# Convolution and ReGLU feed-forward: a smaller tap load spread by TensorE, constants moved to GpSimd, and zero matmuls between the first stages

## The chip, the cores and the metric

The kernel runs on one core of a Trainium2 chip. The metric is the device time of one execution in microseconds, as the median of several runs; lower is better. Durations and times of day inside the kernel come from one profiled execution and count from the start of its span.

## The reference

The input is `x` with 8 sequences of 4096 tokens and 192 channels, all in float32. There are two parts.

1. A causal convolution with 7 taps. The channels form 8 heads of 24; each head has its own 7 taps, which are the soft-max of a row of `weight` (8 rows of 7). Every token becomes the weighted sum of itself and the six tokens before it.
2. A feed-forward layer on all 32768 tokens: `gate = max(x @ w_gate, 0)`, `val = x @ w_val`, both 192 by 1536, and `out = (gate * val) @ w_out`, 1536 by 192.

```python
w = exp(weight - max(weight)); w = w / (sum(w) + 1e-09)
out = einsum('hk,bskhg->bshg', w, x_unfolded)
gate = maximum(x @ w_gate, 0.0)
val = x @ w_val
return gate * val @ w_out
```

## The kernel before

**Tiling.** Two sequences, `NB` = 4 apart, are worked on together as two streams: channels lie on partitions 0 to 63 for one and 64 to 127 for the other, in three chunks of 64 channels. A unit is 1024 tokens of both streams; there are 16 units. In each, `gate_val` runs twice (two windows of 512 tokens) over 12 slices of 128 columns of the two weight matrices: 12 matmuls into PSUM (L521), the relu on ScalarE (`gr`, L530) and the product on VectorE (`hT`, L531). Then `project_columns` multiplies by `Wo` (L541), VectorE turns the result (`turn_out`, L555) and SyncE stores it. The last unit uses `project` (L577) instead. PSUM is one ring of four tiles, all called `ps`.

**The convolution** is made in two ways. From unit 2 on it is done with the taps as per-partition scalars (the "lanes"): GpSimd loads x as float16 (`x_e`, L393), copies it into another order (`x_p`, L430), SyncE turns it with DMA transposes (`x_r`, L425 and L432), ScalarE makes products (`acc` L478, `prod` L458), VectorE accumulates (L489) and GpSimd adds (L467). This is worked on two units ahead: the lanes of unit 2 are made while unit 0 is projected. They need `tap`, the taps laid out by channel, which `load_taps` fills with 32 small DMAs on SyncE (L288) out of `wn`, the taps spread over 16 partitions per head.

For units 0 and 1 the convolution is a matmul with a band matrix. The tokens are cut into groups of up to five steps of 112. Group 0 (`conv_dense(0)`, L325) is on the way to the first gate; group 1 (`conv_dense(1)`) is done between the gates f = 9, 10 and 11 of unit 0; groups 2 and 3 (`conv`, L347) make unit 1.

**The start.** Group 0 of x is read as float32 by SyncE (`load_raw`, L111), one DMA per step in the order `STEPS0` = 1, 0, 2, 3, 4; these are the "raw steps". They are cast to float16 by `cast` (L121): steps 1, 0 and 2 on ScalarE, 3 and 4 on VectorE. The taps are read by ScalarE's queue (L129), with each of the 8 rows repeated for 16 partitions. VectorE and ScalarE make the soft-max (L221, L224, L239, L240) and from it `blocks` (L242). 16 small matmuls (L259) with shifted parts of `Z`, a 0/1 matrix, raise the blocks into the two halves of the band; VectorE copies out the first, ScalarE the second (L269). Ahead of this TensorE runs six matmuls on zeros (`WARM`, L175) and two that zero the band's PSUM (L180).

**Weights.** GpSimd loads both weight matrices in five slices (`load_w`, L198; columns 0, 128, 256, 512, 896 to 1536), cast to float16 on the way, into partitions 0 to 63. The copies to partitions 64 to 127 (`both_halves`, L205) are made by VectorE for slice 0, by GpSimd for slices 1 to 4 (`pool_halves`), and by two SyncE DMAs for the last 256 columns (they lie in load slice 4), at the head of `load_taps`.

**What sets the order.** Each engine takes its instructions in program order, and the order is written by hand. On SyncE it is: raw steps, the two weight copies of L205, the 32 tap loads, the transposes for `x_r`, the transposes for unit 1 (L379), stores. On GpSimd: constants, ten weight loads, the copies of slices 1 to 4 with the two x loads of group 1 (L94) between them, the x loads of group 2, `x_e`, `Wo`, and so on. A DMA waits for the one that had its semaphore before: each of SyncE and GpSimd has eight. VectorE's eviction of chunk 1 (L335) stands behind the copies of slice 0.

```python
for jj in STEPS0:
    for second in range(2):
        for st in range(2):
            for k2 in range(2): ...   # L325: x step (stationary) by band (moving)
copy = nc.vector.tensor_copy if c == 1 and g == 0 else nc.scalar.copy   # L334
```

Of the kernel before, what the change touches and what calls it, by code (L numbers as in the profile page):

```python
# [8 lines left out]
FP = mybir.dt.float32  # L9
F16 = mybir.dt.float16  # L10
ACTF = mybir.ActivationFunctionType
ALU = mybir.AluOpType
# [3 lines left out]
def kernel(  # L16
# [12 lines left out]
    nc = tc.nc  # L29

    B, S, D = x.shape
    H, KW = weight.shape
    G = D // H
    DFF = moe_w_gate.shape[1]
    PAD = KW - 1
# [7 lines left out]
    STEPS = [4, 5, 4]  # L43
    TAPS = [(6, 5, 4), (3, 2), (1, 0)]
    GSUB = 5
    WARM = 6
    STEPS0 = [1, 0, 2, 3, 4]
    CONV1 = [9, 10, 11]

# [12 lines left out]
    const = ctx.enter_context(tc.tile_pool(name="const", bufs=1))  # L62
# [7 lines left out]
    psum = ctx.enter_context(tc.tile_pool(name="psum", bufs=4, space=bass.MemoryType.PSUM))  # L70
# [5 lines left out]
    def staged(i, j):  # L76
        return stages[i][:, XH * j : XH * (j + 1)]

    def load_x(g, streams=range(2)):


        bp, toks = GROUPS[g]
        xt = staged(g // 3, g % 3).rearrange("p (j s d) -> p j s d", s=2, d=D)
        for st in streams:
            b = bp + NB * st
            last = toks[-1] == S - SUB or toks[-1] - toks[-2] != SUB
            n_full = len(toks) - int(last)
            lo = toks[0] - PAD
            src = bass.AP(
                tensor=x.tensor,  # L90
                offset=x.offset + (b * S + lo) * D,
                ap=[[D, 128], [SUB * D, n_full], [1, D]],
            )
            nc.gpsimd.dma_start(out=xt[:, 0:n_full, st, :], in_=src)  # L94
            if last:
                nc.gpsimd.dma_start(
                    out=xt[0 : SUB + PAD, len(toks) - 1, st, :],
                    in_=x[b, toks[-1] - PAD : toks[-1] + SUB, :],
                )
        return xt  # L100

    xts = {0: staged(0, 0).rearrange("p (j s d) -> p j s d", s=2, d=D)}
    ROWS = [SUB + PAD, 128, 128, 128, 80]
    raw = [
        apool.tile([128, FLAT - LDVE], FP, name=f"prod{jj + 1}")[:, 0 : 2 * D] for jj in range(GSUB)
    ]
# [13 lines left out]
    def cast(copy, jj):  # L120
        copy(  # L121
            out=xts[0][0 : ROWS[jj], jj, :, :].rearrange("p s d -> p (s d)"),
            in_=raw[jj][0 : ROWS[jj], :],
        )

    HR = 128 // H
    BW = HR + PAD
    w = const.tile([128, KW], FP)
    nc.scalar.dma_start(  # L129
        out=w[:],  # L130
        in_=bass.AP(tensor=weight.tensor, offset=weight.offset, ap=[[KW, H], [0, HR], [1, KW]]),
    )
    for jj in STEPS0:
        load_raw(jj)

    zeros = const.tile([128, 512], F16)
    nc.vector.memset(zeros[:], 0.0)
    e = const.tile([128, KW + 1], FP)
    nc.vector.memset(e[:, KW:], 1e-9)
    Z = const.tile([128, 256], F16)  # L140
    nc.vector.memset(Z[:], 0.0)
    nc.vector.memset(raw[0][0:PAD, :], 0.0)
    early = const.tile([128, 1], FP)
    nc.scalar.activation(out=early[:], in_=e[:, KW:], func=ACTF.Exp)

    ones = const.tile([128, 128], FP)
    nc.gpsimd.memset(ones[:], 1.0)
    eye = const.tile([128, 128], FP)
    nc.gpsimd.affine_select(
        out=eye[:],  # L150
        in_=ones[:],
        pattern=[[-1, 128]],
        compare_op=ALU.is_equal,
        fill=0.0,
        base=0,
        channel_multiplier=1,
    )
    mask = const.tile([128, H, 1], FP)
    with nc.allow_low_precision("one of the terms is not zero"):
        nc.vector.tensor_reduce(  # L160
            out=Z[:, 112 : 112 + HR],
            in_=eye[:].rearrange("p (g i) -> p i g", i=HR),
            axis=mybir.AxisListType.X,
            op=ALU.add,
        )
    nc.vector.tensor_reduce(
        out=mask[:, :, 0],
        in_=eye[:].rearrange("p (g i) -> p g i", i=HR),
        axis=mybir.AxisListType.X,
        op=ALU.add,  # L170
    )

    held = psum.tile([128, 2, 512], FP, name="ps")
    for _ in range(WARM):
        nc.tensor.matmul(  # L175
            out=held[:, 0, :], lhsT=zeros[:, 0:128], rhs=zeros[:], start=True, stop=True
        )
    raised = [psum.tile([128, 2, 512], FP, name="ps") for _ in range(2)]
    for half in range(2):
        nc.tensor.matmul(  # L180
            out=raised[half][:, 0, 0 : SUB * H // 2],
            lhsT=zeros[:, 0:128],
            rhs=zeros[:, 0 : SUB * H // 2],
            start=True,
            stop=False,
# [3 lines left out]
    Wg = const.tile([128, NCH, DFF], F16)  # L189
    Wv = const.tile([128, NCH, DFF], F16)  # L190
# [4 lines left out]
    def load_w(s):  # L195
        cols = slice(CUTS[s], CUTS[s + 1])
        for src, dst in ((moe_w_gate, Wg), (moe_w_val, Wv)):
            nc.gpsimd.dma_start(  # L198
                out=dst[0:64, :, cols],
                in_=src.rearrange("(c p) f -> p c f", p=64)[:, :, cols],  # L200
            )

    def both_halves(copy, s, dst):
        cols = slice(HALVES[s], HALVES[s + 1])
        copy(out=dst[64:128, :, cols], in_=dst[0:64, :, cols])  # L205

    def pool_halves(s):
        both_halves(nc.gpsimd.tensor_copy, s, Wg)
        both_halves(nc.gpsimd.tensor_copy, s, Wv)

    for s in range(5):
        load_w(s)
    pool_halves(1)
    xts[1] = load_x(1, [0])
    pool_halves(2)
    pool_halves(3)
    load_x(1, [1])
    pool_halves(4)

    mx = const.tile([128, 1], FP)  # L220
    nc.vector.tensor_reduce(  # L221
        out=mx[:], in_=w[:], axis=mybir.AxisListType.X, op=ALU.max, negate=True
    )
    nc.scalar.activation(out=e[:, 0:KW], in_=w[:], func=ACTF.Exp, bias=mx[:])  # L224
    cast(nc.scalar.copy, 1)
    cast(nc.scalar.copy, 0)
    prod = const.tile([128, BW, KW], FP)
    z0 = Z[:, 112 - PAD : 113 - PAD]
    e0 = e[:, 0:1]
    nc.vector.tensor_tensor(  # L230
        out=prod[:],
        in0=bass.AP(tensor=z0.tensor, offset=z0.offset, ap=[z0.ap[0], [1, BW], [1, KW]]),
        in1=bass.AP(tensor=e0.tensor, offset=e0.offset, ap=[e0.ap[0], [0, BW], [1, KW]]),
        op=ALU.mult,
# [8 lines left out]
        out=blocks[:],  # L243
# [11 lines left out]
    for half, copy in enumerate((nc.vector.tensor_copy, nc.scalar.copy)):  # L255
        for j in range(128 // HR):
            s0 = HR * j - PAD
            lo, hi = max(0, -s0), min(BW, SUB - s0)
            nc.tensor.matmul(  # L259
                out=raised[half][:, 0, 0 : SUB * H // 2].rearrange("p (h t) -> p h t", t=SUB)[  # L260
                    :, :, s0 + lo : s0 + hi
                ],
                lhsT=Z[:, 112 - HR * j : 240 - HR * j],
                rhs=blocks[:, H // 2 * half : H // 2 * (half + 1), lo:hi],
                start=False,
                stop=(j == 128 // HR - 1),
                skip_group_check=True,
            )
        copy(  # L269
            out=bands[half][:].rearrange("p h t -> p (h t)"), in_=raised[half][:, 0, 0 : SUB * H // 2]  # L270
        )
    cast(nc.vector.tensor_copy, 3)
    cast(nc.vector.tensor_copy, 4)

# [21 lines left out]
    def band(h):  # L296
        return bands[h // 4][0 : SUB + PAD, h % 4, :]
# [8 lines left out]
    def conv_dense(g, chunks):  # L306


        xt = xts[g]
        t0 = GROUPS[g][1][0]  # L310
        rows = SUB + PAD
        for c in chunks:
            ps = psum.tile([128, 2, 512], FP, name="ps")
            for jj in STEPS0:
                col = SUB * jj
                n = min(SUB, WIN - col)
                rows = n + PAD
                for second in range(2):
                    for st in range(2):
                        for k2 in range(2):  # L320
                            k = 2 * c + k2
                            h0, h1 = 32 * k // G, (32 * k + 31) // G
                            h, m = (h0, G * h1 - 32 * k) if second else (h1, 32)
                            p0 = 64 * st + 32 * k2
                            nc.tensor.matmul(  # L325
                                out=ps[p0 : p0 + m, 0, col : col + n],
                                lhsT=xt[0:rows, jj, st, 32 * k : 32 * k + m],
                                rhs=band(h)[0:rows, 0:n],
                                start=True,
                                stop=True,  # L330
                                tile_position=(0, p0),
                                skip_group_check=True,
                            )
            copy = nc.vector.tensor_copy if c == 1 and g == 0 else nc.scalar.copy  # L334
            copy(out=xc[0][:, c, t0 : t0 + WIN], in_=ps[:, 0, :])  # L335
# [261 lines left out]
    xc[0] = xcpool.tile([128, NCH, UNIT], F16, name="xc")  # L597
    both_halves(nc.vector.tensor_copy, 0, Wg)
    both_halves(nc.vector.tensor_copy, 0, Wv)
    conv_dense(0, range(NCH))  # L600
    xts[2] = load_x(2)
    lane_load(2)
    nc.gpsimd.dma_start(out=Wo[:], in_=moe_w_out.rearrange("(c p) d -> p c d", p=128))
    for u in range(NUNIT):
# [33 lines left out]
        for p in range(3):  # L638
            ps = project_columns(hs, p)
# [39 lines left out]
```

## Time and profile before

| what | us |
|---|---|
| median of 3 runs | 774.18 (773.86 to 775.16) |
| the profiled execution, its own time | 772.72 |
| its span | 771.0 |
| TensorE busy | 761.9 (99%) |
| VectorE busy | 669.8 (87%) |
| ScalarE busy | 598.1 (78%) |
| GpSimd busy | 422.5 (55%) |
| taps land, L221 starts | 4.78 |
| first gate matmul (L521) | 10.88 |
| last x_r of unit 2 lands | 50.26 |

A page of the profile lists busy time per engine, the chain that ended last (followed back from the last instruction; start, duration, engine or queue and line), and groups of instructions. PE is TensorE's matmuls, PEld its weight loads, DVE VectorE, ACT ScalarE, POOL GpSimd, and SPq the issues of SyncE's DMA queue. In a timeline a row has start, duration, engine, line, operation, what is written and read, and in brackets the idle time before it with what ended it. In a view of waits a row has who waited for whom, the total in microseconds, how many times, and the longest. In a table of windows a row has the window, its length, the busy time and count of PE, PEld, DVE, ACT and POOL, the granted TensorE clock, the share of the DMA engines and GB/s.

### The profile page before, as it was taken

Reading aid. Unit: us, or ns where it says so; the run is one execution under the profiler, and the core shown is the slowest. Engines: PE = TensorE matmul, PEld = TensorE weight load, DVE = VectorE, ACT = ScalarE, POOL = GpSimd, SP = SyncE. Lnnn points to the kernel's source line nnn. Section 1 sums busy time; section 2 is a strip of 40 time slices with the busy share of each in tenths; the row PEclk is TensorE's granted clock in tenths of the full one; section 3 lists DMA queues with packets and bytes.
Section 4 is the critical chain, followed back from the end, with each engine's and each line's share of the span. In section 5 each row is a group of like instructions: output and inputs, shape, how many; then the busy total and the mean of one; then the engine's idle time right before and its main releaser. Section 6 shows DMA issues by size and latency. Waiting matters only on the chain.

```text
span 771.0 us, 21553 instructions
## 1 busy us (share of the span) xinstructions
PE 761.9 (99%) x9400; PEld 379.8 (49%) x9400; DVE 669.8 (87%) x630; ACT 598.1 (78%) x622; POOL 422.5 (55%) x189
## 2 busy tenths in 40 slices
PE   7998999999999999999999999999999999999998
PEld 4554544444444444444444444444444444444448
DVE  5878989989899898999989899898998989996691
ACT  5878787978879787787877879788797877874471
POOL 9405839377391955909468292763919558091000
PEclk9999999999999999999999999999999999999999
DMA  9935919075290933709156090742909232040402
GB/s 145 126 66 99 122 24 153 2 107 59 43 125 2 133 33 73 94 3 142 24 91 76 17 150 2 113 55 41 125 3 133 33 72 55 2 82 3 82 2 83
DMA packets 123558, 53.80 MB, mean 70 GB/s; under 512 B 87992, under 2 KB 123464, under 8 KB 123464
## 3 DMA queue, kind: packets, MB, share of 16 engines
q1 hardware_dynamic: 86416, 38.06, 30.3%
q0 software_dynamic: 36768, 14.26, 18.0%
q8 instruction: 73, 1.20, 0.7%
q14 instruction: 21, 0.17, 0.1%
q10 hardware_dynamic: 280, 0.10, 0.0%
HBM read 29.41 MB, written 25.17 MB: 71 GB/s over the span
## 4 chain that ended last, share of the span: by engine, by line
PE 91%; SPq 3%; DMA 3%; ACT 2%; issue 0%; DVE 0%
PE ps L521 60%; PE ps L541 28%; PE ps L577 2%; DMA tap<-wn 2%; ACT prod L458 2%; SPq L288 1%; SPq L432 1%; DMA prod<-in_x_dram 1%; DMA x_r<-x_p 0%; ACT gr L530 0%; PE ps L325 0%; SPq L111 0%; ACT out_s L360 0%; ACT acc L478 0%; SPq L425 0%
## 5 line engine op out<-in xcount | busy, mean ns | idle before, releaser
L530 ACT ACTIVATE gr<-ps 128x1024 f16<-128x1024 f32 x384 | 392.7, 1023 | 145.2 <-PE ps L521 145.2
L531 DVE TENSOR_TENSOR hT<-gr,ps 128x1024 f16<-128x1024 f16 x384 | 468.7, 1221 | 41.2 <-ACT gr L530 14.8
L467 POOL TENSOR_TENSOR prod<-prod,prod 128x1792 f32<-128x1792 f32 x70 | 278.4, 3977 | 259.2 <-DVE prod L499 211.0
L521 PE MATMUL ps<-xc,Wg 64*128 64x512 f16 x2304 | 312.6, 376 | 1.0 <-ACT gr L530 1.0
L521 PE MATMUL ps<-xc,Wv 64*128 64x512 f16 x2304 | 312.3, 376 | 1.2 <-DVE hT L531 0.6
L541 PE MATMUL ps<-hT,Wo 128*32 128x512 f16 x4320 | 236.0, 379 | 0.0
L521 PEld LDWEIGHTS <-Wv 64*128 64x128 f16 x2304 | 130.3, 94 | 120.0 <-issue 1.6
L521 PEld LDWEIGHTS <-Wg 64*128 64x128 f16 x2304 | 112.2, 94 | 138.6 <-issue 7.9
L541 PEld LDWEIGHTS <-Wo 128*32 128x32 f16 x4320 | 114.1, 97 | 120.3 <-issue 6.3
L458 ACT ACTIVATE prod<-x_r,tap 128x1024 f32<-128x1024 f16 (+1 forms) x182 | 172.8, 1039 | 0.0
L489 DVE SCALAR_TENSOR_TENSOR acc<-x_r,tap,acc 128x1024 f32<-128x1024 f16 (+1 forms) x140 | 113.9, 872 | 7.0 <-DMA xc<-out_s 5.0
L555 DVE STREAM_TRANSPOSE out_s<-ps 128x1024 f32<-128x1024 f32 x45 | 56.1, 1247 | 30.7 <-PE ps L541 30.7
L467 POOL TENSOR_TENSOR xc<-prod,prod 128x1792 f16<-128x1792 f32 x14 | 55.7, 3982 | 1.1
L430 POOL COPY x_p<-x_e 128x1536 f16<-128x1536 f16 x28 | 40.3, 1463 | 2.5 <-DMA x_e<-in_x_dram 2.5
L393 POOL DMA_DIRECT2D x_e<-in_x_dram x28 | 25.1, 900 | 4.2 <-POOL x_p L430 4.2
L478 ACT ACTIVATE acc<-x_r,tap 128x1024 f32<-128x1024 f16 (+1 forms) x28 | 21.5, 819 | 5.0 <-DMA x_r<-x_p 5.0
L489 DVE SCALAR_TENSOR_TENSOR xc<-x_r,tap,acc 128x1024 f16<-128x1024 f16 (+1 forms) x28 | 23.4, 878 | 0.0
L577 PE MATMUL ps<-Wo,hT 128*128 128x192 f16 x192 | 16.0, 246 | 0.0
L577 PEld LDWEIGHTS <-hT 128*128 128x128 f16 x192 | 15.8, 98 | 0.4 <-issue 0.4
L588 ACT COPY out_s<-ps 128x768 f32<-128x768 f32 (+2 forms) x5 | 3.2, 638 | 12.7 <-PE ps L577 12.7
L588 DVE COPY out_s<-ps 128x192 f32<-128x192 f32 x1 | 0.4, 358 | 13.3 <-PE ps L577 13.3
L499 DVE TENSOR_SCALAR prod<-x_r,tap 128x768 f32<-128x768 f16 x14 | 8.6, 613 | 0.0
(52 smaller groups left out, 61.4 us busy)
## 6 DMA issues: line engine op xcount, KB each, us to landing
out_dram<-out_s SPq DMA_DIRECT2D x63, 384.0 KB
x_e<-in_x_dram POOLq DMA_DIRECT2D x28, 384.0 KB, 9.8
x_r<-x_p SPq DMA_TRANSPOSE x112
out_s<-in_x_dram POOLq DMA_DIRECT2D x4, 240.0 KB, 5.0
prod<-in_x_dram SPq DMA_DIRECT2D x3, 192.0 KB
Wo<-in_moe_w_out_dram POOLq DMA_DIRECT2D x1, 576.0 KB, 10.8
out_s<-in_x_dram POOLq DMA_DIRECT2D x2, 192.0 KB, 4.4
tap<-wn SPq DMA_DIRECT2D x16, 0.4 KB
```

What stands on the lines that cost most here:

```text
L393: nc.gpsimd.dma_start(out=xe[:, :, st, :, :].rearrange("p j c r -> p j (c r)"), in_=bass.AP(tensor=x.tensor, offset=x.offset + row * D, ap ...
L430: nc.gpsimd.tensor_copy(out=xp[:, :, :, st, :], in_=xe[:, :, st, :, :])
L458: nc.scalar.activation(out=prods[u, k][:, at - LDVE : at - LDVE + n], in_=shifted(u, c, k, t, n), func=ACTF.Copy, scale=tap[:, c, k : k + 1],)
L467: nc.gpsimd.tensor_tensor(out=p0[:] if k < KW - 1 else flat(u)[:, LDVE:FLAT], in0=p0[:], in1=prods.pop((u, k))[:], op=ALU.add,)
L478: nc.scalar.activation(out=accs[u][:, at : at + n], in_=shifted(u, c, 0, t, n), func=ACTF.Copy, scale=tap[:, c, 0:1],)
L489: nc.vector.scalar_tensor_tensor(out=(flat(u) if k == KW - 1 else acc)[:, at : at + n], in0=shifted(u, c, k, t, n), scalar=tap[:, c, k : k ...
L521: nc.tensor.matmul(out=pss[i][:, st, :], lhsT=W[64 * st : 64 * st + 64, c, 128 * f : 128 * (f + 1)], rhs=xcb[64 * st : 64 * st + 64, c, WI ...
L530: nc.scalar.activation(out=gr[:], in_=pss[0][:], func=ACTF.Relu)
L531: nc.vector.tensor_tensor(out=h[:, f], in0=gr[:], in1=pss[1][:], op=ALU.mult)
L541: nc.tensor.matmul(out=ps[32 * s : 32 * s + 32, b, :], lhsT=Wo[:, f, 64 * p + 32 * b : 64 * p + 32 * b + 32], rhs=hs[s // 2][:, f, s % 2, ...
L555: nc.vector.transpose(out=o[:, :, 64 * p : 64 * p + 64].rearrange("p t (b c) -> p b t c", b=2), in_=ps[:].rearrange("p b (t c) -> p b t c" ...
L577: nc.tensor.matmul(out=ps[:, i // 2, D * (i % 2) : D * (i % 2) + D], lhsT=h[:, f, st, 128 * q : 128 * (q + 1)], rhs=Wo[:, f, :], start=(f ...
```

## The change

- The taps are read as 8 rows (`w8`). GpSimd makes `rows8`, an 8 by 128 matrix of 0 and 1 with a 1 where column p belongs to head p // 16, and one float32 matmul spreads the raw rows over 128 partitions into a PSUM tile, `spread`, that VectorE's maximum and ScalarE's exponential read in place of `w`.
- Setting `Z` and the first six raw rows to zero goes from VectorE to GpSimd, ahead of its weight loads, along with the new select.
- The six zero matmuls become 2 ahead of the spreading matmul, 3 behind it, and 1 behind the matmuls of the band.
- The copies of slice 1 go from GpSimd to VectorE, behind those of slice 0, and both x loads of group 1 go behind GpSimd's copies of slice 3.

```diff
-    WARM = 6
+    WARM = [2, 3, 1]
...
-    w = const.tile([128, KW], FP)
-    nc.scalar.dma_start(
-        out=w[:],
-        in_=bass.AP(tensor=weight.tensor, offset=weight.offset, ap=[[KW, H], [0, HR], [1, KW]]),
-    )
+    w8 = const.tile([H, KW], FP)
+    nc.scalar.dma_start(out=w8[:], in_=weight)
...
-    Z = const.tile([128, 256], F16)
-    nc.vector.memset(Z[:], 0.0)
-    nc.vector.memset(raw[0][0:PAD, :], 0.0)
...
+    def select(out, n, pattern):
+        nc.gpsimd.affine_select(
+            out=out,
+            in_=ones[0:n, :],
+            pattern=pattern,
+            compare_op=ALU.is_equal,
+            fill=0.0,
+            base=0,
+            channel_multiplier=1,
+        )
+
+    rows8 = const.tile([H, 128], FP)
+    select(rows8[:], H, [[-1, H], [0, HR]])
     eye = const.tile([128, 128], FP)
...
+    select(eye[:], 128, [[-1, 128]])
+    Z = const.tile([128, 256], F16)
+    nc.gpsimd.memset(Z[:], 0.0)
+    nc.gpsimd.memset(raw[0][0:PAD, :], 0.0)
...
+    def hold(n):
+        for _ in range(n):
+            nc.tensor.matmul(
+                out=held[:, 0, :], lhsT=zeros[:, 0:128], rhs=zeros[:], start=True, stop=True
+            )
+
+    spread = psum.tile([128, 2, 512], FP, name="ps")
+    hold(WARM[0])
+    nc.tensor.matmul(out=spread[:, 0, 0:KW], lhsT=rows8[:], rhs=w8[:], start=True, stop=True)
+    hold(WARM[1])
...
-    pool_halves(1)
-    xts[1] = load_x(1, [0])
     pool_halves(2)
     pool_halves(3)
-    load_x(1, [1])
+    xts[1] = load_x(1)
     pool_halves(4)
...
-        out=mx[:], in_=w[:], axis=mybir.AxisListType.X, op=ALU.max, negate=True
+        out=mx[:], in_=spread[:, 0, 0:KW], axis=mybir.AxisListType.X, op=ALU.max, negate=True
...
-    nc.scalar.activation(out=e[:, 0:KW], in_=w[:], func=ACTF.Exp, bias=mx[:])
+    nc.scalar.activation(out=e[:, 0:KW], in_=spread[:, 0, 0:KW], func=ACTF.Exp, bias=mx[:])
...
+    hold(WARM[2])
     cast(nc.vector.tensor_copy, 3)
...
     both_halves(nc.vector.tensor_copy, 0, Wv)
+    both_halves(nc.vector.tensor_copy, 1, Wg)
+    both_halves(nc.vector.tensor_copy, 1, Wv)
     conv_dense(0, range(NCH))
```

More of the change, by code (lines that the diff above doesn't have):

```diff
@@ L147 @@
     nc.gpsimd.memset(ones[:], 1.0)
-    eye = const.tile([128, 128], FP)
[L149 to L157, printed above, removed]
+    def select(out, n, pattern):
[10 more added lines that the diff above has]
+    select(rows8[:], H, [[-1, H], [0, HR]])
+    eye = const.tile([128, 128], FP)
+    select(eye[:], 128, [[-1, 128]])
+    Z = const.tile([128, 256], F16)
+    nc.gpsimd.memset(Z[:], 0.0)
+    nc.gpsimd.memset(raw[0][0:PAD, :], 0.0)
     mask = const.tile([128, H, 1], FP)
@@ L173 @@
     held = psum.tile([128, 2, 512], FP, name="ps")
[L174 to L177, printed above, removed]
+    def hold(n):
[7 more added lines that the diff above has]
+    hold(WARM[1])
     raised = [psum.tile([128, 2, 512], FP, name="ps") for _ in range(2)]
```

## The prediction, made before the changed kernel was run

> **What bounds the kernel now.** I read the page first (TensorE busy for 761.9 of 771.0 us, so at most 9.1 us are to be had), then the chain that ended last, to see what those 9.1 us hang on:
>
> ```profile
> 8.94 2.01 PE ps L325 x82
> 10.94 1.43 PE ps L521 x10
> ...
> 12.40 1.95 ACT gr L530 x2
> 14.35 0.40 SPq L288
> ...
> 47.20 3.06 DMA x_r<-x_p
> ...
> 50.29 1.55 ACT acc L478 x2
> ...
> 65.94 0.92 ACT gr L530
> ...
> 66.88 1.23 DVE hT L531
> 68.15 28.02 PE ps L521 x258
> ```
>
> From 68.15 us the chain is TensorE alone to the end: what comes before that point shifts the end one to one, what comes after is fixed. But between 14 and 50 us the chain runs through SyncE's queue (SPq), not through TensorE. TensorE meets it again only at 65 to 68 us, in the timeline of TensorE (the bracket is the idle time ahead of the row):
>
> ```profile
> 65.12 0.82 PE L521 MATMUL ps<-xc,Wv 64*128 64x512 f16 x6 [0.57 <-DVE out_s L555]
> 66.89 0.82 PE L521 MATMUL ps<-xc,Wg 64*128 64x512 f16 x6 [0.95 <-ACT gr L530]
> 68.15 0.82 PE L521 MATMUL ps<-xc,Wv 64*128 64x512 f16 x6 [0.43 <-DVE hT L531]
> ```
>
> So TensorE stands 0.57 + 0.95 + 0.43 = 1.95 us here, because ScalarE, which sat idle for 2.94 us until x_r had landed at 50.26, then works without a gap on the taps of unit 2 up to 65.94 before it takes the relu of unit 1. A head that ends sooner on TensorE alone makes this stall longer and nothing else. Next I looked at what SyncE does, in its timeline, and at what it waits for, in the view of waits:
>
> ```profile
> 12.21 0.72 SPq L205 DMA_DIRECT2D Wg<-Wg  x1
> 13.42 0.60 SPq L205 DMA_DIRECT2D Wv<-Wv  x1
> 14.14 22.29 SPq L288 DMA_DIRECT2D tap<-wn  x32
> ...
> 38.15 11.01 SPq L432 DMA_TRANSPOSE x_r<-x_p  x8
> ...
> SPq L205 <- DMA Wg<-in_moe_w_gate_dram: 8.9, 1, 8.9
> SPq L288 <- DMA tap<-wn: 1.8, 3, 0.8
> SPq L205 <- DMA Wv<-in_moe_w_val_dram: 0.5, 1, 0.5
> ```
>
> SyncE issues without a gap from 13.42 to 49.2, except for 1.8 us in which it waits for taps to land, and it starts at 13.42 because the last weight load (Wv, slice 4) lands at 13.40 in the trace's landing records. The chain's own step "gr to L288 at 14.35" is not the cause: that issue had begun at 14.14, straight behind L205. So the time hangs on two things: when the last Wv slice lands, and how long 32 tap loads take.
>
> **The change part by part.**
>
> *GpSimd ahead of its weight issues.* Added: a select of 8 rows (at most the 0.29 of the present select), Z (0.20, the row of `ones`, the same 512 bytes per partition) and the 6 raw rows (0.38, VectorE's row). Sum 0.87: the first weight issue (L198) goes from 1.44 to 2.3. The two memsets come off VectorE, which waited 2.69 us for the taps there, so that is worth nothing. Behind them stand the ten weight issues of 0.63; the tenth waits for slice 0's Wv to land (7.67) and ended at 8.58, so with eight issues done by 7.5 the last ends at 8.7, 0.1 later, and most of the 0.87 is caught up there.
>
> *The tap load.* 128 rows of 28 bytes become 8. Its issue took 1.20 us on ScalarE; SyncE's tap issues took 0.51 to 0.77. It landed at 4.76. Bounds for the landing: 2.6 (the first tap load of SyncE took 1.80 from issue to landing) and 4.7 (unchanged); I take 3.1, near raw step 1, issued at the same moment and landed at 3.45. What else it frees is seen in the windows of 1 us (the last two columns: DMA share, GB/s):
>
> ```profile
> 2.00:3.00 1.00, 1.00 (x4) 0.36 (x3) 0.10 (x1) 0.95 (x1) 1.00 (x3) 1.00 0.82 207
> 3.00:4.00 1.00, 1.00 (x4) 0.40 (x3) 0.00 (x0) 0.53 (x2) 1.00 (x2) 1.00 0.53 55
> 4.00:5.00 1.00, 0.72 (x3) 0.15 (x1) 0.16 (x1) 0.02 (x1) 1.00 (x3) 1.00 0.76 161
> ...
> 8.00:9.00 1.00, 0.92 (x40) 0.55 (x38) 0.81 (x3) 0.03 (x1) 0.74 (x2) 0.50 1.39 195
> ```
>
> Between 3 and 4.5 us the DMA engines move little, while the packets of the 128 tap rows trickle from 2.58 to 4.42 and raw step 0, the second to be issued, stands still. By 0.5 us bins of the packets, in bytes read, that stretch moved 121 KB where the 116 KB per bin ahead of it would give 348: 227 KB lost. Full flow is 200 KB per bin (9 to 12 us), so without the lull everything behind it lands 0.57 sooner. Bounds: −0.57, and +0.3 where the lull has another cause and GpSimd's 0.87 is only partly made good. I take −0.5: the lull and the tap packets coincide, and weights (two bytes written for four read) hardly flow before 4.5 anyway, so the later issue costs little.
>
> *The spread and the soft-max.* The fp32 matmul is in no row; bounds 0.05 (L259: 0.73 for 16) and 0.43 (a 512 wide zero matmul, 2.74 for 6); I take 0.3. Max at 3.4 instead of 4.78, blocks (1.90 behind it) at 5.4 instead of 6.68, first band at 6.6 instead of 7.83. Then the raw steps decide: steps 3 and 4 land at 8.04 and 8.50 now, by 7.5 and 8.0 without the lull.
>
> *VectorE copies slice 1.* Two more copies of 0.57 and 0.52 (the rows of slice 0), both ahead of its eviction of the second chunk at L335, which waits for them, and TensorE's second chunk of the first gate waits for that. VectorE: casts done 8.4, four copies to 10.5, eviction 0.69 to 11.2, against 10.83 now. If slice 1 lands late (8.87 now) this is the wait to see. So the head on TensorE comes out between 0.4 late (no lull removed) and 0.8 early.
>
> *Zero matmuls in the waits.* One more fits into the 0.43 in front of the convolution, the others into the 2.02 ahead of L259. They cost nothing while these gaps last, and 0.21 to 0.43 each if not. The profile's clock is 0.50 from 8 to 11 us, after that gap: 88 matmuls of L325 took 1.93 (8.94 to 10.87), where 40 take 0.57 (23.25 to 23.82) at clock 1.00, so a full clock gives 0.7 there and 0.3 in the first gates. [...]
>
> *GpSimd's order.* Slice 1's copies (1.0) leave it; both x loads of group 1 go behind slice 3. Slice 2's copies start when it lands (9.10 now, 8.6), then 1.53 + 2.19 of copies, 1.74 of x issues from 12.6, slice 4's 2.18: group 2's x load is issued at 16.5 instead of 17.41, and all x and Wo traffic behind it ends about 0.9 sooner (29.5 instead of 30.4). Group 1 is needed at 23.25 − 0.8 and lands by 18: hidden.
>
> *SyncE's tap rounds.* Taps reuse 8 semaphores, so the ninth waits for the first. Eight issues take 5.26 (14.14 to 19.40); the rounds from 19.40 and 25.40 took 6.0 each, because a tap lands 6 us after its issue beside x traffic; the last took 5.0. With traffic ending 0.9 sooner and the taps 0.5 sooner, the third wait (0.48) falls away; the other two stay.
>
> **Sum.** −0.5 (last weight slice) − 0.5 (one tap wait) = −1.0 on x_r, and so on ScalarE at 65.94 and on the end. TensorE's head may come 0.8 sooner as well; 1.95 − 1.0 + 0.8 of stall stays. Against the profiled run (span 771.0, time 772.72) that is 770.0 and 771.7; the median of the runs shown, 774.18, lies 1.46 above it, so 773.2.
>
> **Rivals.** (a) *More:* x traffic leaves before the second and third round, so all 1.8 of tap waits go: −0.57 − 1.8 = −2.4, 771.8. TensorE's own path would allow 1.95 + 0.8 = 2.75. For it: GpSimd's x issues are earlier throughout; against: 10 us of traffic still lie over two rounds. (b) *The lull stays:* weights land −0.1 to +0.3, tap waits as now or 0.48 less: −0.4 to +0.3, 774.1. (c) *Slower:* group 1's x loads now run from 14 to 17 us, under the first tap round. If a tap there lands 6.0 after issue, as in rounds two and three, and so too in the last, beside group 3's loads, the rounds cost 6.0 − 5.26 + 6.0 − 5.0 = +1.74: 775.9. It decides from the point where the first tap takes over 5.26 to land. Against: in the 16 to 18 us stretch, with such a load, taps landed 2.5 to 3.8 after issue. (d) *The head sets the end:* 773.2 to 773.4; the stall at 65 us speaks against it.
>
> **Chances.** Forecast 0.42 (own range 772.5 to 774.0), (a) 0.30, (b) 0.08, (c) 0.18, (d) 0.02. About 0.2% (1.55 us) is what a measurement of this kernel can tell from no change: faster is (a) and 0.03 of the forecast's edge, 0.33; slower is (c), 0.18; the rest, 0.49, is within. 771.7 to 775.9 reaches to the prices of (a) and (c); about 0.12 of (a) and 0.09 of (c) lie beyond them.
>
> **What will show it.** L205's Wv copy on SyncE starts at 12.9, not 13.42; the DMA share at 3 to 4 us is above 0.53; x_r has landed by 49.3 (50.26 now); the stall at 65 us is still above 1 us; SyncE's wait for taps is 1.3 or less. Wrong if the last weight slice lands after 13.4, if the tap waits grow, or if the stall is gone and the head sets the end.

## The result, and the profile after

The changed kernel took 775.26 us (median of 20 runs, 772.91 to 777.51); the kernel before, run beside it, took 773.42 (20 runs, 772.13 to 775.16). The ratio is 1.002 with a 95% interval of 1.0011 to 1.0029: a little slower, where no measurable change was forecast (773.2). The profiled execution of after took 775.43, its span is 773.7, against 772.72 and 771.0 of before: 2.7 us more.

Lines have moved: SyncE's weight copies are L215 (L205 before), the taps L297 (L288), the transposes L441 (L432), the gate matmuls L530 (L521), the relu L539 (L530), the weight issues L208 (L198).

The chain that ended last, after:

```profile
8.83 1.30 PE ps L530 x10
...
49.26 2.35 DMA x_r<-x_p
51.63 1.55 ACT acc L487 x2
...
67.28 0.92 ACT gr L539
68.22 1.23 DVE hT L540
69.49 29.38 PE ps L530 x258
```

The links are those of before, and two numbers make up all the 2.7. ScalarE's `acc` starts at 51.63 (50.29 before), and everything up to TensorE's last restart, 69.49 (68.15), is later by the same 1.34. Then the same 258 matmuls take 29.38 where they took 28.02: 1.36 more. The first half is found in SyncE's timeline:

```profile
13.83 0.72 SPq L215 DMA_DIRECT2D Wg<-Wg  x1
15.05 0.60 SPq L215 DMA_DIRECT2D Wv<-Wv  x1
15.77 22.00 SPq L297 DMA_DIRECT2D tap<-wn  x32
37.87 1.20 SPq L434 DMA_TRANSPOSE x_r<-turned  x1
39.18 11.33 SPq L441 DMA_TRANSPOSE x_r<-x_p  x8
```

The copy of Wv starts at 15.05, 1.63 later than before, as slice 4 of Wv lands at 15.03 instead of 13.40. The taps take 22.00 (22.29), the transposes 11.33 (11.01), and so the end of the transposes is 1.35 later. The view of waits has the same two queues:

```profile
SPq L215 <- DMA Wg<-in_moe_w_gate_dram: 10.5, 1, 10.5
...
SPq L297 <- DMA tap<-wn: 0.2, 1, 0.2
```

SyncE waits 10.5 for the weights (8.9 before) and no longer for taps (0.2, 1.8 before). What happened between issue and landing is on GpSimd's timeline and in the DMA issues (the last column is the time from issue to landing), first of after:

```profile
1.63 0.30 POOL L159 MEMSET Z<- 128x256 f16 x1
1.88 0.41 POOL L160 MEMSET prod<- 6x384 f32 x1
2.25 0.83 POOL L208 DMA_DIRECT2D Wg<-in_moe_w_gate_dram  x1
...
8.07 0.63 POOL L208 DMA_DIRECT2D Wv<-in_moe_w_val_dram  x1
```

```profile
Wv<-in_moe_w_val_dram POOLq DMA_DIRECT2D x1, 240.0 KB, 7.0
```

and of before:

```profile
Wv<-in_moe_w_val_dram POOLq DMA_DIRECT2D x1, 240.0 KB, 5.5
```

The first weight issue moves from 1.44 to 2.25, the tenth only from 7.95 to 8.07, just as the prediction had it. But the last slice then takes 7.0 from issue to landing instead of 5.5. Later issue is 0.12 of the 1.63, slower travel 1.51. The trace's landing records show that this befalls the last slice alone: slice 1 lands at 7.56 and 7.76 (8.70 and 8.87 before), slice 2 at 8.10 and 9.34 (9.10 and 9.57), slice 3 at 10.30 and 11.01 (10.27 and 10.99), and only slice 4 is late, 13.81 and 15.03 (12.20 and 13.40).

The second half is the clock. TensorE's timeline of after, around the first gate and the stall, and then windows (the last three columns: granted clock, DMA share, GB/s):

```profile
8.76 0.39 PE L530 MATMUL ps<-xc,Wg 64*128 64x512 f16 x2
...
57.30 5.36 PE L550 MATMUL ps<-hT,Wo 128*32 128x512 f16 x96 [2.23 <-DVE out_s L564]
...
66.45 0.82 PE L530 MATMUL ps<-xc,Wv 64*128 64x512 f16 x6 [1.74 <-DVE out_s L564]
68.24 0.89 PE L530 MATMUL ps<-xc,Wg 64*128 64x512 f16 x6 [0.96 <-ACT gr L539]
69.49 1.47 PE L530 MATMUL ps<-xc,Wv 64*128 64x512 f16 x6 [0.37 <-DVE hT L540]
```

```profile
3.00:4.00 1.00, 1.00 (x3) 0.30 (x2) 0.63 (x4) 0.74 (x2) 1.00 (x3) 1.00 0.87 217
...
9.00:12.00 3.00, 3.00 (x30) 1.53 (x27) 1.03 (x2) 2.32 (x3) 2.98 (x4) 1.00 1.08 161
...
68.00:70.00 2.00, 1.39 (x10) 0.57 (x11) 1.78 (x2) 1.93 (x3) 2.00 (x1) 0.72 0.27 55
70.00:72.00 2.00, 2.00 (x12) 0.75 (x10) 1.51 (x2) 0.19 (x1) 2.00 (x2) 0.50 0.99 186
```

The same windows of before:

```profile
9.00:12.00 3.00, 3.00 (x98) 2.26 (x100) 1.62 (x3) 1.17 (x2) 3.00 (x5) 0.60 1.24 206
...
70.00:72.00 2.00, 2.00 (x22) 1.01 (x18) 1.58 (x2) 1.70 (x2) 1.99 (x3) 1.00 0.98 184
```

The first gate starts at 8.76 instead of 10.88, 2.1 sooner. None of it reaches the end: TensorE comes sooner to a point that lies later, and stands 2.23 + 1.74 + 0.96 + 0.37 = 5.3 us where it stood 1.95. In that quiet stretch the granted clock falls to 0.50 (0.72 from 68 to 70, 0.50 from 70 to 72), and 12 matmuls are done in 2 us where before 22 were. The trace's clock records put the half clock at 68.87 to 72.29, 3.42 us. That the longer stall is what closes the clock is not shown; set 3 has traces that speak against it. The window at 9 to 12 us shows the DMA engines moving 161 GB/s (206 before), just when the last weights are under way; the lull at 3 to 4 is gone (217 GB/s, 55 before).

### The profile page after: what moved, and what is told of

It is laid out like the page before. It is cut to its first block, busy times and chain, and to the rows that moved or that the text cites. A ratio compares the mean times of both kernels' runs of the same rounds, so it can differ in the third digit from the quotient of the medians.

```text
span 773.7 us, 21558 instructions
## 1 busy us (share of the span) xinstructions
PE 763.6 (99%) x9402; PEld 380.1 (49%) x9402; DVE 669.3 (86%) x630; ACT 598.0 (77%) x622; POOL 422.5 (55%) x190
## 4 chain that ended last, share of the span: by engine, by line
PE 91%; SPq 3%; ACT 2%; DMA 2%; issue 0%; DVE 0%
PE ps L530 61%; PE ps L550 28%; PE ps L586 2%; SPq L297 2%; ACT prod L467 1%; SPq L441 1%; DMA tap<-wn 1%; DMA prod<-in_x_dram 1%; ACT gr L539 0%; DVE hT L540 0%; DMA x_r<-x_p 0%; ACT out_s L369 0%; ACT acc L487 0%; PE ps L334 0%; SPq L111 0%
## 5 line engine op out<-in xcount | busy, mean ns | idle before, releaser
L539 ACT ACTIVATE gr<-ps 128x1024 f16<-128x1024 f32 x384 | 392.6, 1023 | 148.1 <-PE ps L530 147.7
L530 PE MATMUL ps<-xc,Wv 64*128 64x512 f16 x2304 | 313.0, 377 | 2.3 <-DVE out_s L564 1.7
L530 PE MATMUL ps<-xc,Wg 64*128 64x512 f16 x2304 | 313.1, 377 | 1.0 <-ACT gr L539 1.0
L530 PEld LDWEIGHTS <-Wv 64*128 64x128 f16 x2304 | 130.7, 94 | 121.4 <-issue 4.2
L530 PEld LDWEIGHTS <-Wg 64*128 64x128 f16 x2304 | 112.2, 94 | 139.3 <-issue 8.6
```

The costliest lines, as they stand in the source:

```text
L530: nc.tensor.matmul(out=pss[i][:, st, :], lhsT=W[64 * st : 64 * st + 64, c, 128 * f : 128 * (f + 1)], rhs=xcb[64 * st : 64 * st + 64, c, WI ...
L539: nc.scalar.activation(out=gr[:], in_=pss[0][:], func=ACTF.Relu)
```

## The experiments

All kernels compute the whole reference; some add useless work, named below. Ratios are against the kernel before, run beside them on the same chip, with 95% intervals. The theory after this result: the two memsets ahead of GpSimd's weight issues make the last slice late, and SyncE's chain takes it to the end. Rivals: the new order of GpSimd's copies and x loads; the zero matmuls and the longer stall; the tap load itself.

### Set 1: which part costs

**The memsets back on VectorE** (all else as after; first weight issue 1.64):

```diff
-    nc.gpsimd.memset(Z[:], 0.0)
-    nc.gpsimd.memset(raw[0][0:PAD, :], 0.0)
+    nc.vector.memset(Z[:], 0.0)
+    nc.vector.memset(raw[0][0:PAD, :], 0.0)   # both ahead of `early`
```

> The changed kernel with the two memsets (Z and the six raw rows) back on VectorE; GpSimd has only the 8-row select ahead of its weight issues, so the first one is at about 1.6 us instead of 2.25. Theory A (GpSimd's delay makes the last weight slice late, and with it SyncE's L215, x_r and the end): the Wv copy on SyncE starts by 14.3 us or sooner instead of 15.05, and the time is 0.6 to 1.4 us below the changed kernel's. Theory B (the new order of GpSimd's copies and x loads, or VectorE's copies, make it late): start and time as in the changed kernel, 15.0 us and 775.3 us. Theory C (the rate of the weight DMAs varies from run to run and the constants have no part in it): the start lies anywhere between 13 and 15.

773.62, ratio 0.9997 (0.9988 to 1.0005), 1.64 below after where 0.6 to 1.4 was expected. SyncE's timeline:

```profile
13.38 0.60 SPq L215 DMA_DIRECT2D Wv<-Wv  x1
```

Two memsets of 0.30 and 0.41 decide: 1.64 of the 1.84 us are gone, and the interval does not touch that of after. The slice lands at 13.36 again in this trace.

**The order of GpSimd's work back** (slice 1 and the x loads of group 1 as before):

```diff
+    pool_halves(1)
+    xts[1] = load_x(1, [0])
     pool_halves(2)
     pool_halves(3)
-    xts[1] = load_x(1)
+    load_x(1, [1])
     pool_halves(4)
...
-    both_halves(nc.vector.tensor_copy, 1, Wg)
-    both_halves(nc.vector.tensor_copy, 1, Wv)
```

> The changed kernel with slice 1 copied by GpSimd again and one x load of group 1 between slices 1 and 2, as before; constants, tap load and zero matmuls as changed. Theory A: SyncE's Wv copy still starts at 14.5 us or later and the time stays within 0.5 us of the changed kernel's. Theory B: it starts at 13.4 to 13.9 again and the time falls by 1.2 us or more.

774.63, 1.0021 (1.0006 to 1.0036), 0.63 below after, a little outside the 0.5 expected. The Wv copy starts at 15.97, later still, in a trace that is the slowest of its 12 runs (778.07):

```profile
15.97 0.60 SPq L215 DMA_DIRECT2D Wv<-Wv  x1
```

So the order of copies and x loads is not what delays the slice.

**The constants alone** (the kernel before, with the select and the two memsets on GpSimd; the select's output is not used, the taps are read as before):

```diff
-    nc.vector.memset(Z[:], 0.0)
-    nc.vector.memset(raw[0][0:PAD, :], 0.0)
+    # on GpSimd, behind eye and ahead of the weight loads
+    nc.gpsimd.affine_select(out=rows8[:], in_=ones[0:H, :], ...)
+    nc.gpsimd.memset(Z[:], 0.0)
+    nc.gpsimd.memset(raw[0][0:PAD, :], 0.0)
```

> The kernel before with one part of the change alone: both memsets and an unused 8-row select on GpSimd ahead of its weight issues. Theory A: SyncE's Wv copy starts at 14.2 to 15.0 us instead of 13.42 and the time is 0.8 to 1.5 us above the kernel before. Theory B and C: start at 13.4 to 13.7, time within 0.3 us of the kernel before.

774.57, 1.0016 (1.0002 to 1.0031):

```profile
14.63 0.60 SPq L215 DMA_DIRECT2D Wv<-Wv  x1
```

This one part, put into the kernel before, delays the Wv copy by 1.21, and the median is 1.15 above that of before, most of the loss, with no other part of the change there. The profiled execution is the fastest of the 12 (773.15); in it only 0.40 of the 1.21 is left at `acc`, which starts at 50.69.

**Filler ahead of the first gate** (after, with ten useless zero matmuls of 512 columns, which take the head's gain away):

```diff
+            if u == 0 and w == 0 and f == 0:
+                for _ in range(10):
+                    nc.tensor.matmul(out=pss[0][:, 0, :], lhsT=zeros[:, 0:128], rhs=zeros[:], ...)
```

> The changed kernel with ten useless 512 wide zero matmuls ahead of the first gate, which hold TensorE up by about 2.1 us at the head and change nothing on GpSimd, SyncE or the DMAs. Theory A with the clock (the end is set by SyncE's chain; TensorE coming early only lengthens its stall at 55 to 69 us, and a stall that long shuts the clock for 3.4 us, 1.4 us lost, in some runs): the time is not above the changed kernel's and up to 1.4 us below it; the clock is 1.00 from 55 to 75 us. Rival (the head counts): 2.1 us slower than the changed kernel.

775.02, 1.0013 (1.0003 to 1.0022): 2.1 us of useless work on TensorE in the head cost nothing; they shorten the stall. In TensorE's timeline 1.32 + 0.96 + 0.43 = 2.71 is left of 5.3 (`acc` also starts 1.0 sooner in this trace, at 50.62), and the clock stays at 1.00:

```profile
65.45 0.82 PE L535 MATMUL ps<-xc,Wv 64*128 64x512 f16 x6 [1.32 <-DVE out_s L569]
67.24 0.82 PE L535 MATMUL ps<-xc,Wg 64*128 64x512 f16 x6 [0.96 <-ACT gr L544]
68.49 0.82 PE L535 MATMUL ps<-xc,Wv 64*128 64x512 f16 x6 [0.43 <-DVE hT L545]
```

Over 12 runs it is 0.24 better than after, too little to tell from nothing.

### Set 2: the chain cut, and the dose doubled

If the slice counts only because 32 taps stand behind its copies on SyncE, then taps put ahead of the copies make it harmless. **Fourteen taps first**, on after and on before (`FIRST` = 14), and on the version with the memsets back:

```diff
-        both_halves(nc.sync.dma_start, 5, Wg)
-        both_halves(nc.sync.dma_start, 5, Wv)
...
+                        if n_tap == FIRST:
+                            both_halves(nc.sync.dma_start, 5, Wg)
+                            both_halves(nc.sync.dma_start, 5, Wv)
+                        n_tap += 1
```

> The changed kernel with one thing else: on SyncE the first 14 tap loads go ahead of the two weight copies of L215, the other 18 behind them. The taps then no longer wait for the last weight slice. Theory A (SyncE's chain from that slice to x_r sets the end): SyncE's first tap load starts at about 5 us instead of 15.8, x_r of unit 2 lands by 46 us instead of 51.6 (it then waits for x_p, copied by GpSimd until 31.5), TensorE's stall at 55 to 69 us shrinks from 5.3 to under 1 us, and the time falls by 4 to 6 us, to 769 to 771. Rival (the end hangs on the head or on the weights themselves): within 1 us of the changed kernel's 775.3.

> The kernel before with the same order of SyncE's queue. Theory A: only the stall of 1.95 us at 65 us can be won, so 1.5 to 2.2 us faster than the kernel before, 771.2 to 771.9, and slower than the changed kernel in the same order by about the 2.1 us that the change saves at the head. Rival: no difference.

> Both at once: memsets back on VectorE and the first 14 taps ahead of L215. Theory A: once the taps no longer wait for the last slice, its landing costs nothing, so this is within 0.5 us of the changed kernel with the taps first. If the late slice costs in another way too (slices for the gates of unit 0), this one is faster by that.

On after 769.7, ratio 0.9941 (0.9929 to 0.9953); on before 770.93, 0.9956 (0.9945 to 0.9968); with the memsets back 769.33, 0.9939 (0.9927 to 0.995), **the best version, ahead of both kernels by 4 to 6 us**. SyncE's timeline, what is left of TensorE's stall, and one link of the chain, on after:

```profile
4.75 10.63 SPq L301 DMA_DIRECT2D tap<-wn  x14
15.50 0.72 SPq L215 DMA_DIRECT2D Wg<-Wg  x1
16.32 0.64 SPq L215 DMA_DIRECT2D Wv<-Wv  x1
17.01 13.20 SPq L301 DMA_DIRECT2D tap<-wn  x18
```

```profile
63.77 0.82 PE L534 MATMUL ps<-xc,Wg 64*128 64x512 f16 x6 [0.64 <-ACT gr L543]
65.03 0.82 PE L534 MATMUL ps<-xc,Wv 64*128 64x512 f16 x6 [0.43 <-DVE hT L544]
```

```profile
65.03 28.02 PE ps L534 x258
```

The slice lands at 15.91, later than in after, and nobody minds: SyncE no longer stands idle for 10 us, `acc` starts at 47.17 instead of 51.63 (x_r was expected by 46), TensorE's stall is 0.64 + 0.43 = 1.07 instead of 5.3 (under 1 expected), and its chain begins at 65.03. That shows that SyncE's order, not TensorE's head, sets the end of after and of before. The head gain now counts for something: after with this edit is 1.2 us faster than before with it, though the intervals of the ratios just overlap. About 2.1 was expected; before with this edit has no stall left in its trace, after still has the 1.07. On before the edit won more than expected, 770.93 where 771.2 to 771.9 was forecast from a stall of 1.95: a second trace of before (set 3) stands for 1.66 + 0.96 + 0.43 = 3.05, so there was more to win.

**The delay doubled** (after, with two more useless GpSimd memsets of 128x384 ahead of the weight loads; first weight issue 2.97):

```diff
+    idle = const.tile([128, 2, 384], FP)
+    for i in range(2):
+        nc.gpsimd.memset(idle[:, i, :], 0.0)
```

> The changed kernel with two more useless memsets on GpSimd (384 float32 a partition each) ahead of the weight issues, which go from 2.25 to about 3.0 us. Theory A: the last weight slice lands 0.7 us or more later again (15.5 us or later), and the time grows by 0.7 to 1.5 us over the changed kernel's, to 776.0 to 776.8. Theory C (chance): no shift beyond 0.4 us.

776.78, 1.0038 (1.0024 to 1.0051). The Wv copy is at 15.57, `acc` at 55.37, and nearly all of TensorE's stall is one piece, with the clock at 0.50 from 60.13 to 66.96, so that the 96 matmuls behind it take 8.26 instead of 5.36:

```profile
61.04 8.26 PE L553 MATMUL ps<-hT,Wo 128*32 128x512 f16 x96 [5.30 <-DVE out_s L567]
```

The median grows with the delay, by 1.5, though the interval overlaps that of after (1.0011 to 1.0029). The landing grew less (0.5) than `acc` (3.7): further down, SyncE's tap issues and transposes are later too.

### Set 3: the remaining parts, and the spread between executions

**The tap load alone** (8 rows and the spreading matmul; memsets, order and copies as before, `WARM` = [2, 0, 0]) and **no zero matmuls** (after with `WARM` = [2, 0, 0]), and one more profiled execution of each kernel:

```diff
-    WARM = [2, 3, 1]
+    WARM = [2, 0, 0]
```

> One part of the change alone: the taps read as 8 rows and spread by the matmul (with its 8-row select on GpSimd), the rest as before (memsets on VectorE, GpSimd's copies and x loads in the old order, two zero matmuls ahead and none in the waits). Theory A: TensorE's first gate matmul comes 0.5 to 1.5 us sooner than 10.88, the last weight slice lands within 0.5 us of 13.4, and the time is within 0.6 us of the kernel before: what the head wins is absorbed. Rival (the head counts): 0.5 to 1.5 us faster than the kernel before.

> The changed kernel without the zero matmuls in the waits (two ahead of the spreading matmul, none behind it). Theory A: the granted clock is 0.50 in part of the 6 to 12 us stretch and the first gate matmul comes later than 8.76 by up to 1 us, but the time is the changed kernel's, within 0.6 us or less, since the end hangs on SyncE's chain. Rival (the head counts): up to 1 us slower than the changed kernel.

> The kernel before once more, for a second trace: the last weight slice lands at 13.4 within 0.5 us if that landing is the kernel's own (theory A), anywhere between 13 and 15 if it varies by chance (theory C).

> The changed kernel once more, for a second trace: the last slice lands at 13.9 us or later (theory A), anywhere between 13 and 15 by theory C. [...]

The tap load alone: 773.66, 1.0003 (0.999 to 1.0015); first gate 9.94, 0.9 sooner than before, and nothing won. Without the zero matmuls: 774.81, 1.0015 (1.0007 to 1.0024); the first gate is at 9.58, so they had bought 0.8 of head, and 0.45 is gained by leaving them out, within the noise. The granted clock was expected at 0.50 somewhere from 6 to 12 us; the profile has 1.00 there. The matmuls are slower all the same, and the pairs of the first gate start every 0.42 us instead of 0.22; first without the zero matmuls, then in after:

```profile
7.21 2.44 PE L334 MATMUL ps<-band,out_s 118*32 118x112 f16 x96 [0.24 <-DVE out_s L121]
9.58 0.61 PE L530 MATMUL ps<-xc,Wg 64*128 64x512 f16 x2
```

```profile
7.39 1.44 PE L334 MATMUL ps<-band,out_s 118*32 118x112 f16 x96 [0.23 <-DVE out_s L121]
```

The second profiled executions: after has its Wv copy at 14.43 (774.41), before at 14.42 (775.2). The last is a miss: it was to be within 0.5 of 13.4, and is 1.0 off. The landing of the last slice varies between executions of one kernel by up to a microsecond, so that a single landing settles nothing, and the verdicts rest on the medians.

The second trace of after also bears on what closes the clock. Its stall is 1.93 + 1.74 + 0.96 + 0.43 = 5.06, nearly that of the first, and the clock stays at 1.00. With the memsets back on VectorE the stall is 0.91 + 0.96 + 0.18 = 2.05, and the clock is at 0.50 from 67.85 to 71.26. First the stall and a window of the second trace of after, then the same with the memsets back:

```profile
56.97 5.36 PE L550 MATMUL ps<-hT,Wo 128*32 128x512 f16 x96 [1.93 <-DVE out_s L564]
...
66.12 0.82 PE L530 MATMUL ps<-xc,Wv 64*128 64x512 f16 x6 [1.74 <-DVE out_s L564]
67.91 0.82 PE L530 MATMUL ps<-xc,Wg 64*128 64x512 f16 x6 [0.96 <-ACT gr L539]
69.17 0.82 PE L530 MATMUL ps<-xc,Wv 64*128 64x512 f16 x6 [0.43 <-DVE hT L540]
...
68.00:70.00 2.00, 1.57 (x14) 0.67 (x15) 2.00 (x2) 1.79 (x2) 2.00 (x1) 1.00 0.29 59
```

```profile
65.63 0.82 PE L530 MATMUL ps<-xc,Wv 64*128 64x512 f16 x6 [0.91 <-DVE out_s L564]
67.41 1.08 PE L530 MATMUL ps<-xc,Wg 64*128 64x512 f16 x6 [0.96 <-ACT gr L539]
68.67 1.46 PE L530 MATMUL ps<-xc,Wv 64*128 64x512 f16 x6 [0.18 <-DVE hT L540]
...
68.00:70.00 2.00, 1.82 (x12) 0.56 (x9) 1.75 (x2) 1.29 (x2) 2.00 (x1) 0.50 0.57 111
```

So the length of the stall does not decide whether the clock falls, nor does its longest single piece: with the memsets back none is over 0.96, and in the second trace of after one is 1.93. The clock also fell after 2.50 with the tap load alone, and did not after 3.14 with the constants alone or 3.05 in the second trace of before.

### Set 4: is it GpSimd's time, or the head start?

Why should 0.7 us ahead of the first issue matter, if the last issue is at the same time? In the kernel before, 0.6 to 0.7 us of useless GpSimd work was put ahead of the first weight issue, behind slice 0, and ahead of slice 4's issues:

```diff
+    idle = const.tile([128, 2, 384], FP)
     for s in range(5):
+        if s == POS:              # 0, 1 or 4
+            for i in range(2):
+                nc.gpsimd.memset(idle[:, i, :], 0.0)
         load_w(s)
```

> The kernel before with 0.75 us of useless memsets on GpSimd ahead of the first weight issue. As with the constants alone: weights flow at 160 KB/us or less between 9 and 12 us, the last slice lands at 14.2 us or later, and the time is 0.8 to 1.5 us above the kernel before. If it costs nothing, the memsets of the change are not the cause but something tied to Z or the raw rows.

> The same 0.75 us behind slice 0, ahead of the third weight issue. If only the head start of the first issue counts: flow 200 KB/us from 9 to 12 us, no loss beyond 0.3 us. If the later issues' lead over the flow counts: slower flow, 0.5 us or more lost.

> The same 0.75 us ahead of the ninth issue, where GpSimd waits 0.6 to 0.96 us for slice 0 to land anyway. The wait hides it: flow 200 KB/us, time within 0.3 us of the kernel before. If the delay as such costs: 0.7 us or more lost.

Ahead of all: 774.24, 1.001 (1.0001 to 1.0019). Behind slice 0: 773.9, 1.0006 (0.9998 to 1.0015). Ahead of slice 4: 773.53, 1.0003 (0.9994 to 1.0012). The last issue begins at 8.08, 8.02 and 8.04, and the Wv copy at 14.03, 14.03 and 13.22. The first was expected to cost 0.8 to 1.5 with the slice landing at 14.2 or later; it costs 0.47 against before run beside it (773.77), and the slice lands at 14.01. In the middle one, 192 GB/s flow from 9 to 12 us, and GpSimd waits 0.84 for slice 1 ahead of its copies; it has no measurable loss, though its Wv copy is as late as the first one's. Windows of the first and of the last (last two columns: DMA share, GB/s):

```profile
9.00:12.00 3.00, 3.00 (x79) 1.97 (x70) 0.69 (x1) 1.41 (x3) 3.00 (x5) 1.00 0.91 131
```

```profile
9.00:12.00 3.00, 3.00 (x96) 2.20 (x95) 1.49 (x3) 1.17 (x2) 3.00 (x5) 0.53 1.23 206
```

The flow tells the same work early (131) from the same work late (206). The medians point the same way, but their intervals overlap, so that the head start of GpSimd's queue, and not GpSimd's time, is likely rather than shown. Put in a row by the first weight issue, with all that did not move the taps (copy, flow and `acc` from one trace each):

| first weight issue (us) | kernels | Wv copy starts (us) | GB/s at 9 to 12 us | `acc` starts (us) | median (us) | ratio |
|---|---|---|---|---|---|---|
| 1.44 | before, second trace; delay ahead of slice 4; delay behind slice 0 | 13.42, 14.42; 13.22; 14.03 | 206, 205; 206; 192 | 50.29, 51.79; 50.66; 51.88 | 773.42; 773.53; 773.9 | 1; 1.0003; 1.0006 |
| 1.64 | memsets back; tap load alone | 13.38; 13.88 | 181; 178 | 50.80; 51.25 | 773.62; 773.66 | 0.9997; 1.0003 |
| 2.04 | delay ahead of all | 14.03 | 131 | 50.58 | 774.24 | 1.001 |
| 2.25 | after, second trace; constants alone; order back; filler; no zero matmuls | 15.05, 14.43; 14.63; 15.97; 13.93; 14.60 | 161, 150; 149; 162; 154; 128 | 51.63, 51.30; 50.69; 55.61; 50.62; 51.26 | 775.26; 774.57; 774.63; 775.02; 774.81 | 1.002; 1.0016; 1.0021; 1.0013; 1.0015 |
| 2.97 | delay doubled | 15.57 | 118 | 55.37 | 776.78 | 1.0038 |

The flow of the weights sorts the kernels without an overlap: 192 to 206 GB/s, 178 to 181, and 118 to 162 from an issue at 2.04 on. The start of the Wv copy and of `acc` in single traces do not, so the step from slower flow to lost time rests on the medians and on set 2, not on these columns.

## Why the prediction was wrong, point by point

- **What bounds the kernel: right.** The chain from the last weight slice over SyncE's taps to `acc`, the stall and TensorE was read correctly, and so was "a head that ends sooner on TensorE alone makes this stall longer": the filler's 2.1 us cost nothing, and cutting the chain gave 4 us. "What comes after is fixed" held only where the clock stayed at 1.00, as said below.
- **"GpSimd ahead of its weight issues": the step that failed.** Its issue times were right (first 2.3, last ending 8.7; measured 2.25 and 8.70). "Most of the 0.87 is caught up there" took the time of the last issue for the time of the last landing. The issues catch up, the last slice does not: it travelled 7.0 instead of 5.5 us. The sum had −0.5 for it; measured at the Wv copy: +1.63 in the profiled run, +1.21 with the constants alone.
- **"The tap load", everything behind it 0.5 sooner: wrong for the weights, right for x.** The lull went, as forecast, and raw steps 0 and 4 landed at 3.99 and 7.19 (5.42 and 8.50). The 128 tap rows are only part of its cause: the constants alone, with the 128 rows but the weights issued 0.8 later, move 159 GB/s at 3 to 4 us (55 before) and land step 4 at 7.01. So the later weight issue itself lets x through. In after slices 1 and 2 came sooner too, by 0.2 to 1.1, but the last slice, on which the −0.5 was booked, did not even without the memsets: 13.36 and 13.88 against 13.40. From "weights hardly flow before 4.5" the prediction took that a later issue is cheap; the flow of 131 GB/s behind an early delay and 206 behind a late one speaks against that, and so do the medians of the memsets back and of the constants alone.
- **The soft-max and the head: better than priced.** Head forecast 0.4 late to 0.8 early; measured 2.1 early. The soft-max began at 2.91 instead of the forecast 3.4, though the two passes of the spreading matmul ran 0.56 in all, above the bound of 0.43 (the row named for it, 2.74 for 6, gives 0.46); the zero matmuls gave 0.8 of the 2.1 (first gate at 9.58 without them, 8.76 with them) by the pace of the matmuls behind them, with the granted clock at 1.00 in both traces; and the four copies on VectorE took 0.27 to 0.29 each, not the 0.57 and 0.52 taken from before. The prediction had 0.7 + 0.3 for a full clock in the head, and rival (d)'s 773.2 rests on it. That zero matmuls raise the granted clock was the author's estimate, and no run shows it: the second trace of before has 1.00 from 8 to 12 us with none of them in those waits.
- **The tap waits: −0.5 in the sum, −0.29 measured.** The waits fell by 1.6 (1.8 to 0.2), more than forecast, but the 32 issues took 22.00 against 22.29: without waits, 21.8 against 20.5, so most of it came back as longer issues.
- **A term put at nothing: the clock behind the stall.** In the profiled run the clock fell to 0.50 in the stall, for 3.42 us and at a price of 1.36. The prediction looked at the clock behind the gap before the convolution and not behind the stall. That the change causes it is not shown: the clock stayed at 1.00 in a stall of 5.06 and fell in one of 2.05, and what decides it stays open. So does its share of the median. The 11 runs of after at a clock of 1.00 have a median of 774.37, the 9 below it 775.38; for before the same two groups have 773.42 and 773.45 beside the first set, 772.96 and 774.05 beside the second. The filler's 8 runs at 1.00 still have 774.98, so a large part of the loss needs no fall of the clock.
- **The sum.** −1.0 forecast on `acc`, +1.34 measured; 0 forecast behind the stall, +1.36 measured; together +2.7 in the profiled pair, +1.84 between the medians. The profiled pair is luck in part: the second traces of the two kernels have spans of 772.7 (after) and 773.5 (before), the other way round.
- **The rivals.** (a) died with the late slice: the tap waits did go, but 773.7, not 768.6, was the span. (b) named the right place, weights no sooner, with a bound (+0.3) five times too small. (c), the slower one, gave 775.9, close to what came, but by a mechanism that did not occur: the taps waited less, not more. (d) is refuted by the filler.

**What stays open.** Why the weights flow more slowly at 9 to 12 us when their first issue was 0.6 to 0.8 us later and their last at most 0.3. Single edits speak against the order of GpSimd's copies and x loads, the zero matmuls, the tap load and GpSimd's time as such. The packet records show what the slower flow is made of: from 7 us to the landing of the last slice, 30 packets of GpSimd's queue took over 0.25 us in after, up to 1.14, but one in before, one in its second trace, and none with the delay ahead of slice 4; with the constants alone and with the delay ahead of all there are 24 each. So single packets are held up; why is not known. VectorE's two additional copies are no explanation, since the constants alone and the delay ahead of all have only the two copies of before and flow as slowly (149 and 131 GB/s, after 161). Whether VectorE's work beside GpSimd's issues has a part in it is neither shown nor excluded: with the constants alone VectorE's copies run from 7.87, while GpSimd issues until 8.63; in before they start at 8.91, behind its last issue (8.58), but VectorE's casts of x lie beside that issue there too, from 8.06. No run tests it. The share of the clock in the median is open as well, as said above.

## What to carry to other kernels

The issue time of a DMA is not its landing (here the last issue came 0.12 later, its landing 1.63): where a queue of weight loads ends on the critical path, keep even 0.7 us of memsets from in front of its first issue, and put such work late among the issues (ahead of slice 4: 773.53, no measurable loss) or on an engine that waits anyway (773.62 with the memsets on VectorE, 775.26 with them on GpSimd). Take more than one trace before naming a cause: here the landing and the clock's price differ between executions of one kernel by 1.0 and 1.4 us, nearly as much as the effect. Follow a saved microsecond down the chain to the instruction that restarts the bound engine: here three good edits to the head bought 2.1 us of longer stall. When one queue idles for 9 us ahead of a transfer that others don't need yet, reorder that queue; moving 14 of 32 small loads in front of the wait was worth more than all parts of the change (ratios 0.9941 on after and 0.9956 on before, against 1.002).

## What the runs showed of the hardware that was not expected

- The weights' last slice took 5.5 us from issue to landing behind a first issue at 1.44, and 7.0 behind one at 2.25, its own issue being 0.12 later.
- 64x384 float16 copies on VectorE took 0.57 and 0.52 in the profile of before, and 0.27 to 0.29 in that of after, where the last ended (8.52) before GpSimd's first copy began at 8.74; in before, GpSimd's copies lay beside them, from 8.84 on. In the version with memsets back and taps first the fourth copy, at 9.12, took 0.84 beside GpSimd's from 8.91; its third, at 8.93, took 0.27 all the same. That copies beside each other are slower was not tested by itself.
- A stall of TensorE can end with the granted clock at 0.50 for 3.42 us, into the matmuls behind it: the same 258 matmuls took 29.38 instead of 28.02. The length of the stall did not decide it: the clock fell in stalls of 2.05 and 2.50 and not in ones of 3.05, 3.14 and 5.06.
- Matmuls can run at half the pace while the profile grants a clock of 1.00: without the zero matmuls ahead of them the pairs of the first gate started every 0.42 us, with them every 0.22.
- The flow of GpSimd's weight loads at 9 to 12 us was 192 to 206 GB/s with the first issue at 1.44, and 118 to 162 with it at 2.04 or later, with single packets of up to 1.14 us in after.
